# Weights stationary instead of tokens stationary in the last products of a two-layer MLP, with the result turned by VectorE

## The chip, the cores and the metric

The kernel runs on one NeuronCore of a Trainium2 chip. The metric is the device time of one execution, in microseconds, as the median of a few runs. The engines are TensorE (PE, with its weight loads as PEld), VectorE (DVE), ScalarE (ACT) and the DMA queue that SyncE (SP) issues. GpSimd does nothing here.

## What is computed

Three stages follow each other over 12160 tokens (2 sequences of 6080) with 256 features: a gated scan along the sequence, an MLP with squared ReLU, and an MLP with ELU. Both MLPs go 256 to 2048 to 256.

```python
f = lb + (1 - lb) * sigmoid(f_logit)
for t in range(S):                       # scan, per sequence and feature
    h = f[:, t] * h + (1 - f[:, t]) * x[:, t]
    y[:, t] = h
x1 = square(relu(y @ moe_w_in)) @ moe_w_out
out = elu(x1 @ moe2_w_in) @ moe2_w_out   # fp32 out, [12160, 256]
```

## The kernel before

**Precision.** Every fp32 operand of a product is split into a high part that TensorE's fp32r format holds and a low part that is the rest. A product is three matmuls: high by high, high by low, low by high.

**Tiling.** Tokens are cut into 24 blocks: one of 384, then 23 of 512 (`block_sizes`). In the code `m` is the MLP (0 or 1), called layer 1 and layer 2 here, `b` the block, `g` one of eight groups of 256 hidden features. A slot is one (m, b, g): first products (x by w_in, L611, in two parts "first" and "later", for a seven-product scheme on half blocks; L625 in the first four blocks of layer 1), the activation on ACT and DVE (lines 639 to 673), the split of the hidden values into `g` high (L678, ACT) and low (L683, DVE), and the second products (`out_mm`, L710), which accumulate over the eight groups in PSUM banks `acc`.

**Second products.** In layer 1 the output weights `wo[0]` are stationary and the 512 tokens of `g` move: per slot 2 hidden chunks x 2 halves of the 256 output features x 3 = 12 matmuls with 512 moving columns. In layer 2 the tokens are stationary (128 at a time) and the 256 columns of `wo[1]` move: per slot 2 x 4 x 3 = 24 matmuls with 256 moving columns (18 in the block of 384). So layer 2's result has tokens on partitions and can be stored as it is.

**Order on TensorE.** The order of PE steps is written out by hand: runs of two blocks of one layer are woven slot by slot, 16 slots to a run. Two runs of layer 1 begin, then runs of layer 2 and layer 1 alternate, and two runs of layer 2 end the kernel. So there are twelve layer-2 runs: a first one (blocks 0 and 1); nine (called the middle runs below) that alternate with layer 1; and a last two that follow each other. A slot's second products come three slots after its first products.

**Order on the other engines.** The class `Order` is a planner: each step has an engine, a cost in us, a due time and the buffers that it reads and writes; it plays the steps through at planning time, and on each engine takes the ready step with the earliest due time. What comes out is a fixed order per engine, in which each engine works strictly.

**After the second products.** `add_evacuation` gives, for each block, two steps per layer. For layer 1, ACT copies each `acc` bank (L775) and SP spills it to DRAM (L778). For layer 2, ACT copies each `acc` bank to a staging tile `o` (L790, two per block) and SP stores it to `out` (L794, rows of 1 KB). There are four `acc` banks (two blocks of a run in flight) and two `o` tiles. The scan (`add_scan`, L541 to L578) loads its inputs in DMAs of 64 KB, four per half block and tensor, and turns them with DVE's 32x32 block transposes (L550).

**Weights.** `add_weights` makes the parts of the output weights once per group: `high_part` (L402 on ACT or L404 on DVE) and `low_part` (L408, DVE), one instruction of 512 columns each.

Of the kernel before, what the change touches and what calls it, by code (L numbers as in the profile page):

```python
# [7 lines left out]
F32 = mybir.dt.float32  # L8
# [7 lines left out]
P = 128  # L16
# [138 lines left out]
def kernel(  # L155
# [24 lines left out]

    late = ctx.enter_context(tc.tile_pool(name="late", bufs=1))
    wo1 = late.tile([P, KF, 2, D], F32R, name="wo1")
    pools = {"ws": ctx.enter_context(tc.tile_pool(name="ws_pool", bufs=BUFS["ws"]))}
    const = ctx.enter_context(tc.tile_pool(name="const", bufs=1))
    lb = const.tile([P, KD], F32, name="lb")
# [1 line left out]
    gb = const.tile([P, KD], F32, name="gb")  # L189
    carry = const.tile([P, KD], F32, name="carry")  # L190
    warm = const.tile([P, 1], F32, name="warm")
    wo = [const.tile([P, KF, 2, D], F32R, name="wo0"), wo1]
    pools |= {
        tag: ctx.enter_context(tc.tile_pool(name=f"{tag}_pool", bufs=n))
        for tag, n in BUFS.items()
# [37 lines left out]
    def new(tag, shape, dtype=F32, name=None):  # L233
        return pools[tag].tile(shape, dtype, tag=name or tag, name=name or tag)
# [54 lines left out]
    def act(n, psum=False):  # L289
        return (0.05 if psum else 0.09) + n / 1172  # L290
# [68 lines left out]
    def add_weights(i, m, kind, c, due, wk=None):  # L359
        t = {}  # L360

        def load(e):
            t["st"] = new("st", [P, 2, CE // 2, 2], I32)
            load_w(nc.scalar if i == 0 else nc.sync, t["st"], m, kind, c)
            if i == 0:
                for k in range(KD):
                    nc.scalar.dma_start(lb[:, k : k + 1], lower_bound.rearrange("(q c i o) -> c q i o", q=4, c=KD, o=1)[k])
                nc.scalar.activation(warm, warm, AF.Exp)
            sv = t["st"].rearrange("p k e w -> p (k e) w")
            t["low"], t["high"] = sv[:, :, 0], sv[:, :, 1]  # L370

        def scaled(e):
            t["a"] = new("a", [P, 4, P])
            t["v"] = t["a"].rearrange("p q i -> p (q i)")
            t["vi"] = t["v"].bitcast(I32)
            nc.scalar.activation(t["v"], t["high"].bitcast(F32), AF.Abs, scale=2.0**-112)

        def low_bits(e):
            nc.scalar.activation(t["low"], t["low"].bitcast(U32), AF.Copy, scale=LOW_SCALE)

        def magnitude(e):
            nc.vector.scalar_tensor_tensor(t["vi"], t["vi"], 3, t["low"], op0=ALU.logical_shift_left, op1=ALU.bitwise_or)

        def sign(e):
            nc.vector.scalar_tensor_tensor(t["vi"], t["high"], -0x80000000, t["vi"], op0=ALU.bitwise_and, op1=ALU.bitwise_or)

        def sums(e):
            t["q"] = new("a", [P, 4, P])
            weight_sums(t["q"], t["a"])

        def parts():
            if kind == 0:
                return t["a"], ws_t[m, c][:, 0, 0:4], ws_t[m, c][:, 1, 0:4]
            v = t["a"].rearrange("p (k e) i -> p k (e i)", k=2)
            return v, *(wo[m][:, 2 * c : 2 * c + 2, x, :] for x in range(2))

        def high_part(e):
            if kind == 0:
                ws_t[m, c] = new("ws", [P, 2, NW, P], F32R)
            v, hi, _ = parts()  # L400
            if e == "ACT":
                nc.scalar.activation(hi, v, AF.Copy)  # L402
            else:
                nc.vector.tensor_copy(hi, v)  # L404

        def low_part(e):
            v, hi, lo = parts()
            nc.vector.tensor_tensor(lo, v, hi.bitcast(F32), op=ALU.subtract)  # L408

        def keep(e):  # L410
            nc.sync.dma_start(wd[m][c][:, :, 0:4].bitcast(F32), ws_t[m, c][:, :, 0:4].bitcast(F32))

        def keep_whole(e):
            nc.sync.dma_start(rd[c], t["a"])

        st, a = ("st", i), key_of("a")
        steps = [
            ["SP", 0.1 if i == 0 else 1.9 if m == 0 and kind == 0 else 0.475, load, (), [st], None, 512],
            ["ACT", act(CE), scaled, [st], [a]],
            ["ACT", act(CE), low_bits, (), [st]],  # L420
            ["DVE", dve(CE), magnitude, [st], [a]],
            ["DVE", dve(CE), sign, [st], [a]],
        ]
        if i == 0:
            order.add(*steps[0][:2], -20.0, *steps[0][2:])
            del steps[0]
        if m == 1 and kind == 0:
            q = key_of("a")
            chain(due - 6.0, [*steps, ["DVE", 4 * dve(P), sums, [a], [q]]])
            add_kept_parts(t, "a", a, m, c, 0, due - 2.0)  # L430
            add_kept_parts(t, "q", q, m, c, 4, due)
            return
        w = ("ws", wk) if kind == 0 else ("w", m, c)
        chain(due, [
            *steps,
            ["DVE", dve(CE, True), high_part, [a], [w], ("ACT", act(CE))],
            ["DVE", dve(CE), low_part, [a], [w]],
        ])
        if kind == 0:
            order.add("SP", 0.5, due + 6.0, keep, [w], [("wd", m, c, 0)], None, 512)  # L440
            order.add("SP", 0.5, due + 3.0, keep_whole, [a], [("rd", c)], None, 256)
# [160 lines left out]
    def add_slot(i, m, b, g, wk):  # L602
# [82 lines left out]
        def out_mm(e):  # L685
            begin, end = g == 0, g == KG - 1
            if begin:
                acc_t[m, b] = []
            for j in (2 * g + 1, 2 * g):
                d = 0 if j % 2 else 2 * n  # L690
                gh, gl = (t["g"][:, x, d : d + 2 * n] for x in range(2))
                one, two = begin and j % 2 == 1, end and j % 2 == 0
                for q in range(KD if m == 0 else 2 * n // P):
                    if m == 0:
                        if one:
                            acc_t[m, b].append(pa.tile([P, TB], F32, tag="acc", name="acc"))
                        a = acc_t[m, b][q][:, : 2 * n]
                        wh, wl = (wo[0][:, j, x, q * P : (q + 1) * P] for x in range(2))
                        three = ((wh, gh), (wh, gl), (wl, gh))
                        clear = one  # L700
                    else:
                        if one and q % 2 == 0:
                            acc_t[m, b].append(pa.tile([P, TB], F32, tag="acc", name="acc"))
                        a = acc_t[m, b][q // 2][:, q % 2 * D : (q % 2 + 1) * D]
                        vh, vl = (x[:, q * P : (q + 1) * P] for x in (gh, gl))
                        wh, wl = (wo[1][:, j, x, :] for x in range(2))
                        three = ((vh, wh), (vh, wl), (vl, wh))
                        clear = one and q % 2 == 0
                    for k, (u, v) in enumerate(three):
                        nc.tensor.matmul(a, lhsT=u, rhs=v, start=clear and k == 0, stop=two and k == 2, skip_group_check=True)  # L710

        na = KD if m == 0 else -(-2 * n // HB)
        if g == 0:
            t0 = acc_n[0]
            acc_n[0] += na
# [50 lines left out]
    def add_evacuation(m, b):  # L766
        n = sizes[b]
        due = out_due[m, b, KG - 1] + 12 * ROW * n + 4.0
        for q, key in enumerate(acc_k[m, b]):
            if m == 0:  # L770
                k = ("o", o_n[0] + q)

                def move(e, q=q):
                    o_t[m, b, q] = new("o", [P, 2, D])[:, :, : n // 2]
                    nc.scalar.activation(o_t[m, b, q], acc_t[m, b][q][:, :n].rearrange("p (h i) -> p h i", h=2), AF.Copy)  # L775

                def spill(e, q=q):
                    nc.sync.dma_start(xd[b][:, q], o_t[m, b, q])  # L778

                chain(due, [  # L780
                    ["ACT", act(n, True), move, [key], [k]],
                    ["SP", 0.5, spill, [k], [("xd", b, q)], None, n // 2],
                ])
            else:
                k = ("o", o_n[0] + q)
                w = min(2, n // P - 2 * q)

                def move(e, q=q, w=w):
                    o_t[m, b, q] = new("o", [P, 2, D])
                    nc.scalar.activation(o_t[m, b, q][:, :w], acc_t[m, b][q].rearrange("p (i e) -> p i e", i=2)[:, :w], AF.Copy)  # L790

                def store(e, q=q, w=w):
                    t0 = starts[b] + q * 2 * P
                    nc.sync.dma_start(out[t0 : t0 + w * P, :].rearrange("(i p) e -> p i e", p=P), o_t[m, b, q][:, :w])  # L794

                chain(due, [
                    ["ACT", act(w * D, True), move, [key], [k]],
                    ["SP", 0.5, store, [k], (), None, w * 128],
                ])
        o_n[0] += len(acc_k[m, b])  # L800

    def add_reload(b, due):
        n = sizes[b] // 2
# [97 lines left out]
```

## Time and profile before

| | us |
|---|---|
| median of 3 runs | 2113.92 (2113.29 to 2114.46) |
| profiled execution, its own time | 2113.18 |
| its span, first to last instruction | 2111.4 |

| engine | busy us | share of the span |
|---|---|---|
| PE | 2041.2 | 97% |
| PEld | 1925.7 | 91% |
| DVE | 1717.8 | 81% |
| ACT | 1692.7 | 80% |

The time outside the span is 1.8 us. Busy time of PE counts matmuls that overlap in the pipeline, so it is read here from starts: the distance from the first matmul of a group to the first of the next. The DVE's and ACT's instructions overlap their neighbours by some 0.08 us too. TensorE's granted clock is 0.997 of full speed over the run.

### The profile page before, as it was taken

The numbers are of one execution on the slowest core, as the hardware profiler recorded it, in microseconds if no ns is written. First come the engines' busy times: TensorE is split into PE (matmuls) and PEld (weight loads), VectorE is DVE, ScalarE is ACT, GpSimd is POOL, SyncE is SP. The second block draws the span as 40 slices with busy tenths as digits, with TensorE's granted clock in tenths as the row PEclk, the third lists the DMA queues.
The fourth block names the chain that finished last, engine by engine and source line by source line (L and its number), as shares of the span: only waits on it lengthen the run. The fifth ranks groups of instructions, "written<-read, shape, count | busy, mean of one in ns | idle before, by whom it ended". The sixth has DMA issues, their size and how long they took to land.

```text
span 2111.4 us, 36876 instructions
## 1 busy us (share of the span) xinstructions
PE 2041.2 (97%) x14640; PEld 1925.7 (91%) x14640; DVE 1717.8 (81%) x2833; ACT 1692.7 (80%) x2146; POOL 0.2 (0%) x4
## 2 busy tenths in 40 slices
PE   3999899999999999999999999999999999999998
PEld 2888889999899899999999989989999998999998
DVE  6977986986987887798698698789879859867886
ACT  5877787887788888788788888878878878878886
POOL 0000000000000000000000000000000000000000
PEclk8999999999999999999999999999999999999999
DMA  7877442432433433333243243333334324323231
GB/s 214 230 261 246 152 149 88 136 130 83 135 118 108 123 113 128 120 105 123 92 142 131 85 138 103 123 118 108 122 117 117 128 88 128 125 90 128 88 108 38
DMA packets 207539, 268.08 MB, mean 127 GB/s; under 512 B 110984, under 2 KB 135944, under 8 KB 207368
## 3 DMA queue, kind: packets, MB, share of 16 engines
q1 hardware_dynamic: 206784, 265.21, 39.9%
q8 instruction: 115, 1.88, 0.4%
q10 hardware_dynamic: 584, 0.53, 0.1%
q14 instruction: 56, 0.46, 0.1%
HBM read 221.91 MB, written 43.78 MB: 126 GB/s over the span
## 4 chain that ended last, share of the span: by engine, by line
PE 71%; DVE 20%; ACT 4%; DMA 2%; issue 2%; SPq 1%; DVEq 0%; ACTq 0%
PE acc L710 38%; PE pc L611 30%; DVE g L683 4%; PE pc L625 4%; DVE r L654 2%; DVE F L576 2%; DVE r L673 2%; DVE s L642 1%; DVE r L650 1%; DVE s L647 1%; DVE fT L559 1%; DMA xs<-in_x_dram 1%; DVE fT L550 1%; DVE xA L508 1%; DVE xT L562 1%
## 5 line engine op out<-in xcount | busy, mean ns | idle before, releaser
L710 PE MATMUL acc<-wo,g 128*128 128x256 f32 x4560 | 584.4, 283 | 20.2 <-DVE g L683 19.9
L710 PEld LDWEIGHTS acc<-wo,g 128*128 128x128 f32 x4560 | 561.3, 188 | 25.9 <-DVE g L683 25.2
L710 PE MATMUL acc<-g,wo 128*128 128x512 f32 (+1 forms) x2304 | 552.2, 389 | 0.0
L611 PE MATMUL pc<-xA,ws 128*128 128x256 f32 (+1 forms) x3696 | 486.1, 280 | 7.1 <-ACT s L639 7.1
L683 DVE TENSOR_TENSOR g<-r,g 128x1024 fp32r<-128x1024 f32 (+1 forms) x384 | 463.6, 1207 | 35.4 <-ACT g L678 34.3
L710 PEld LDWEIGHTS acc<-g,wo 128*128 128x128 f32 x2304 | 420.7, 188 | 78.1
L611 PE MATMUL pc<-xB,ws 128*128 128x256 f32 x3696 | 487.0, 281 | 3.9 <-ACT s L639 3.9
L611 PEld LDWEIGHTS pc<-xA,ws 128*128 128x128 f32 x3696 | 462.1, 188 | 17.0 <-ACT s L639 11.2
L611 PEld LDWEIGHTS pc<-xB,ws 128*128 128x128 f32 x3696 | 463.4, 188 | 11.0 <-ACT s L639 4.6
L678 ACT ACTIVATE g<-r 128x1024 fp32r<-128x1024 f32 (+1 forms) x384 | 403.1, 1050 | 58.3 <-DVE r L673 51.5
L647 DVE TENSOR_TENSOR s<-pc,s 128x256 f32<-128x256 f32 (+1 forms) x352 | 147.7, 420 | 283.5 <-PE pc L611 283.3
L639 ACT ACTIVATE s<-pc 128x768 f32<-128x768 f32 (+1 forms) x352 | 283.1, 804 | 48.8 <-PE pc L611 48.0
L673 DVE SCALAR_TENSOR_TENSOR r<-e,r 128x1024 f32<-128x1024 f32 (+1 forms) x192 | 231.2, 1204 | 22.7 <-ACT e L670 22.7
L654 DVE TENSOR_TENSOR r<-pc,s 128x512 f32<-128x512 f32 (+1 forms) x352 | 241.0, 685 | 7.7 <-ACT r L657 2.6
L657 ACT ACTIVATE r<-pc 128x256 f32<-128x256 f32 (+1 forms) x352 | 134.0, 381 | 112.5 <-DVE r L654 66.4
L660 ACT ACTIVATE r<-r 128x768 f32<-128x768 f32 x160 | 135.6, 847 | 105.3 <-DVE r L650 105.3
L667 ACT ACTIVATE e<-r 128x1024 f32<-128x1024 f32 (+1 forms) x192 | 201.2, 1048 | 19.0 <-DVE r L650 14.6
L663 ACT ACTIVATE r<-r 128x1024 f32<-128x1024 f32 (+1 forms) x192 | 202.1, 1053 | 5.4
L670 ACT ACTIVATE e<-e 128x1024 f32<-128x1024 f32 (+1 forms) x192 | 201.6, 1050 | 5.0
L642 DVE TENSOR_TENSOR s<-s 128x256 f32<-128x256 f32 (+1 forms) x352 | 147.4, 419 | 9.3 <-ACT s L639 0.7
L650 DVE TENSOR_TENSOR r<-s 128x256 f32<-128x256 f32 (+1 forms) x352 | 147.0, 418 | 0.0
L625 PE MATMUL pc<-xA,ws 128*128 128x384 f32 (+1 forms) x192 | 44.0, 382 | 23.2 <-DVE xA L502 22.9
(49 smaller groups left out, 849.5 us busy)
## 6 DMA issues: line engine op xcount, KB each, us to landing
ws<-wd SPq DMA_DIRECT2D x176, 896.0 KB, 5.0
out_dram<-o SPq DMA_DIRECT2D x47, 256.0 KB, 2.4
fs<-in_f_logit_dram SPq DMA_DIRECT2D x184, 64.0 KB, 2.4
xs<-in_x_dram SPq DMA_DIRECT2D x184, 64.0 KB, 2.8
xd<-o SPq DMA_DIRECT2D x46, 256.0 KB, 3.4
F<-xd SPq DMA_DIRECT2D x46, 256.0 KB, 5.0
st<-in_moe_w_out_dram SPq DMA_DIRECT2D x16, 512.0 KB, 4.9
wd<-wp SPq DMA_DIRECT2D x24, 256.0 KB, 4.7
```

What stands on the lines that cost most here:

```text
L611: nc.tensor.matmul(t["pc"][:, c], lhsT=ws[:, p, w], rhs=x_t[m, b][:, r, v], start=(which is FIRST_PRODUCTS and q == 0 and c in (1, 2)), st ...
L639: nc.scalar.activation(t["s"], t["pc"][:, 1:4], AF.Copy)
L642: nc.vector.tensor_tensor(t["s"][:, 1], t["s"][:, 1], t["s"][:, 2], op=ALU.add)
L647: nc.vector.tensor_tensor(t["s"][:, 0], t["pc"][:, 0], t["s"][:, 0], op=ALU.add)
L654: nc.vector.tensor_tensor(t["c"][:, 1:3], t["pc"][:, 2:4], u, op=ALU.add)
L663: nc.scalar.activation(t["r"], t["r"], AF.Square)
L667: nc.scalar.activation(t["e"], t["r"], AF.Relu, scale=-1.0)
L670: nc.scalar.activation(t["e"], t["e"], AF.Exp, scale=-1.0)
L673: nc.vector.scalar_tensor_tensor(t["r"], t["e"], 1.0, t["r"], op0=ALU.subtract, op1=ALU.max)
L678: nc.scalar.activation(t["g"][:, 0], t["r"], AF.Copy)
L683: nc.vector.tensor_tensor(t["g"][:, 1], t["r"], t["g"][:, 0].bitcast(F32), op=ALU.subtract)
L710: nc.tensor.matmul(a, lhsT=u, rhs=v, start=clear and k == 0, stop=two and k == 2, skip_group_check=True)
```

## The change

Layer 2's second products take the form of layer 1's: the weights `wo[1]` are stationary, the tokens of `g` move, 12 matmuls of 512 columns (384 in the first block) instead of 24 (18) of 256. The result then has features on partitions. For each block DVE transposes it from PSUM in blocks of 32x32, four instructions of 256 columns (two halves of the block, each from both `acc` banks), into the staging tile; ACT's two copies per block go away. So that a plain 32x32 block transpose gives 64 features in a row for a token, the columns of `wo[1]` are put in another order when they are made, in two instructions of 256 columns instead of one of 512 for each part. Each half of a block is stored by four DMAs of 64 KB with runs of 256 bytes, instead of one of 256 KB with runs of 1 KB. The tile `wo1` moves to another pool.

```diff
-                return t["a"], ws_t[m, c][:, 0, 0:4], ws_t[m, c][:, 1, 0:4]
+                return [(t["a"], ws_t[m, c][:, 0, 0:4], ws_t[m, c][:, 1, 0:4])]
             v = t["a"].rearrange("p (k e) i -> p k (e i)", k=2)
-            return v, *(wo[m][:, 2 * c : 2 * c + 2, x, :] for x in range(2))
+            hi, lo = (wo[m][:, 2 * c : 2 * c + 2, x, :] for x in range(2))
+            if m == 0:
+                return [(v, hi, lo)]
+            return [
+                (v[:, k].rearrange("p (a q j) -> p q a j", a=4, q=KD),
+                 *(u[:, k].rearrange("p (q a j) -> p q a j", a=4, q=KD) for u in (hi, lo)))
+                for k in range(2)
+            ]
...
-                    else:
-                        if one and q % 2 == 0:
-                            acc_t[m, b].append(pa.tile([P, TB], F32, tag="acc", name="acc"))
-                        a = acc_t[m, b][q // 2][:, q % 2 * D : (q % 2 + 1) * D]
-                        vh, vl = (x[:, q * P : (q + 1) * P] for x in (gh, gl))
-                        wh, wl = (wo[1][:, j, x, :] for x in range(2))
-                        three = ((vh, wh), (vh, wl), (vl, wh))
-                        clear = one and q % 2 == 0
+                for q in range(KD):
+                    if one:
+                        acc_t[m, b].append(pa.tile([P, TB], F32, tag="acc", name="acc"))
+                    a = acc_t[m, b][q][:, : 2 * n]
+                    wh, wl = (wo[m][:, j, x, q * P : (q + 1) * P] for x in range(2))
+                    for k, (u, v) in enumerate(((wh, gh), (wh, gl), (wl, gh))):
+                        nc.tensor.matmul(a, lhsT=u, rhs=v, start=one and k == 0, stop=two and k == 2, skip_group_check=True)
...
-                def move(e, q=q, w=w):
-                    o_t[m, b, q] = new("o", [P, 2, D])
-                    nc.scalar.activation(o_t[m, b, q][:, :w], acc_t[m, b][q].rearrange("p (i e) -> p i e", i=2)[:, :w], AF.Copy)
-                def store(e, q=q, w=w):
-                    t0 = starts[b] + q * 2 * P
-                    nc.sync.dma_start(out[t0 : t0 + w * P, :].rearrange("(i p) e -> p i e", p=P), o_t[m, b, q][:, :w])
+                def turn(e, h=q):
+                    o_t[m, b, h] = o = new("o", [P, HB // 32, KD, 32])[:, : n // 64]
+                    for c in range(KD):
+                        v = acc_t[m, b][c][:, h * n // 2 : (h + 1) * n // 2]
+                        nc.vector.transpose(o[:, :, c], v.rearrange("p (n i) -> p n i", i=32))
+                def store(e, h=q):
+                    t0 = starts[b] + h * n // 2
+                    v = out[t0 : t0 + n // 2, :].rearrange("(n j) (a u) -> a j n u", j=32, a=4)
+                    for a in range(4):
+                        nc.sync.dma_start(v[a], o_t[m, b, h][32 * a : 32 * a + 32].rearrange("j n c i -> j n (c i)"))
                 chain(due, [
-                    ["ACT", act(w * D, True), move, [key], [k]],
-                    ["SP", 0.5, store, [k], (), None, w * 128],
+                    ["DVE", 2 * dve(n // 2), turn, accs, [k]],
+                    ["SP", 1.9, store, [k], (), None, n // 2],
                 ])
```

## Rows read from the trace of the kernel before

**Rows 1.** Page, part 1: busy us (share of the span) x instructions.

```profile
PE 2041.2 (97%) x14640; PEld 1925.7 (91%) x14640; DVE 1717.8 (81%) x2833; ACT 1692.7 (80%) x2146; POOL 0.2 (0%) x4
```

**Rows 2.** Page, part 4: the chain that ended last, share by engine.

```profile
PE 71%; DVE 20%; ACT 4%; DMA 2%; issue 2%; SPq 1%; DVEq 0%; ACTq 0%
```

**Rows 3.** Groups by shape: busy us, mean ns of one, idle before and its releaser.

```profile
L710 PE MATMUL acc<-wo,g 128*128 128x256 f32 x4560 | 584.4, 283 | 20.2 <-DVE g L683 19.9 <-ACT g L678 0.3
L710 PE MATMUL acc<-g,wo 128*128 128x512 f32 x2208 | 535.1, 391 | 0.0
...
L647 DVE TENSOR_TENSOR s<-pc,s 128x256 f32<-128x256 f32 x344 | 144.9, 421 | 282.2 <-PE pc L611 282.0
L642 DVE TENSOR_TENSOR s<-s 128x256 f32<-128x256 f32 x344 | 144.5, 420 | 8.6
...
L550 DVE STREAM_TRANSPOSE xT<-xs 128x512 f32<-128x512 f32 x46 | 32.3, 702 | 0.0
```

**Rows 4.** Timeline of PE in a layer-1 run: start us, us, line, matmuls merged.

```profile
333.24 2.91 PE L710 MATMUL acc<-g,wo 128*128 128x512 f32 x12
335.99 1.57 PE L611 MATMUL pc<-xA,ws 128*128 128x256 f32 x12
...
348.88 1.32 PE L710 MATMUL acc<-g,wo 128*128 128x512 f32 x5
```

**Rows 5.** Timeline of PE in a middle layer-2 run.

```profile
1109.73 3.04 PE L710 MATMUL acc<-wo,g 128*128 128x256 f32 x24
1112.61 1.58 PE L611 MATMUL pc<-xA,ws 128*128 128x256 f32 x12
...
1125.84 3.04 PE L710 MATMUL acc<-wo,g 128*128 128x256 f32 x24
```

**Rows 6.** Waits of the engines: total us, times, longest us.

```profile
PE acc L710 <- DVE g L683: 19.9, 26, 1.0
```

**Rows 7.** Busy us of each engine in stretches: length, PE, PEld, DVE, ACT.

```profile
214.00:307.00 93.00, 84.22 (x692) 82.05 (x691) 91.60 (x169) 72.14 (x102) 0.00 (x0) 1.00 0.49 150
...
461.00:481.00 20.00, 20.00 (x164) 19.73 (x163) 19.11 (x31) 18.37 (x26) 0.00 (x0) 1.00 0.44 148
481.00:533.00 52.00, 52.00 (x331) 47.07 (x330) 29.44 (x51) 40.51 (x51) 0.00 (x0) 1.00 0.25 89
533.00:576.00 43.00, 41.56 (x285) 38.13 (x283) 42.76 (x76) 34.87 (x46) 0.00 (x0) 1.00 0.53 148
...
1941.00:2091.00 150.00, 150.00 (x1260) 150.00 (x1259) 120.41 (x179) 121.61 (x148) 0.00 (x0) 1.00 0.26 89
```

**Rows 8.** Timeline of PE where a layer-2 run begins, with idle before.

```profile
576.75 2.89 PE L710 MATMUL acc<-wo,g 128*128 128x256 f32 x22 [1.02 <-DVE g L683]
```

**Rows 9.** Timeline of DVE where that layer-2 run's predecessor ended.

```profile
465.16 0.41 DVE L642 TENSOR_TENSOR s<-s 128x256 f32<-128x256 f32 x1
465.49 0.42 DVE L650 TENSOR_TENSOR r<-s 128x256 f32<-128x256 f32 x1
...
471.70 0.69 DVE L484 TENSOR_TENSOR F<-F 128x512 f32<-128x512 f32 x1
...
483.84 0.42 DVE L647 TENSOR_TENSOR s<-pc,s 128x256 f32<-128x256 f32 x1 [2.29 <-PE pc L611]
```

**Rows 10.** Timeline of all engines at the end of the kernel.

```profile
2104.71 2.89 PE L710 MATMUL acc<-wo,g 128*128 128x256 f32 x22 [0.75 <-DVE g L683]
2106.93 1.31 ACT L790 ACTIVATE o<-acc 128x512 f32<-128x512 f32 x2 [3.53 <-PE acc L710]
2107.56 1.08 SPq L794 DMA_DIRECT2D out_dram<-o  x2
```

**Rows 11.** Waits of SP's queue: total us, times, longest us.

```profile
SPq L468 <- PE pc L611: 1099.3, 135, 12.2
```

**Rows 12.** Timeline of SP: four 64 KB loads of the scan, issued in a row.

```profile
566.01 1.79 SPq L541 DMA_DIRECT2D xs<-in_x_dram  x4
```

**Rows 13.** Page, part 6: DMA issues, KB each, us from issue to landing.

```profile
fs<-in_f_logit_dram SPq DMA_DIRECT2D x184, 64.0 KB, 2.4
```

More of the change, by code (lines that the diff above doesn't have):

```diff
@@ L179 @@
     NBK = len(sizes)
-    late = ctx.enter_context(tc.tile_pool(name="late", bufs=1))
-    wo1 = late.tile([P, KF, 2, D], F32R, name="wo1")
     pools = {"ws": ctx.enter_context(tc.tile_pool(name="ws_pool", bufs=BUFS["ws"]))}
@@ L191 @@
     warm = const.tile([P, 1], F32, name="warm")
-    wo = [const.tile([P, KF, 2, D], F32R, name="wo0"), wo1]
+    wo = [const.tile([P, KF, 2, D], F32R, name=f"wo{m}") for m in range(2)]
     pools |= {
@@ L399, in high_part @@
                 ws_t[m, c] = new("ws", [P, 2, NW, P], F32R)
-            v, hi, _ = parts()
-            if e == "ACT":
-                nc.scalar.activation(hi, v, AF.Copy)
-            else:
-                nc.vector.tensor_copy(hi, v)
+            for v, hi, _ in parts():
+                if e == "ACT":
+                    nc.scalar.activation(hi, v, AF.Copy)
+                else:
+                    nc.vector.tensor_copy(hi, v)
         def low_part(e):
-            v, hi, lo = parts()
-            nc.vector.tensor_tensor(lo, v, hi.bitcast(F32), op=ALU.subtract)
+            for v, hi, lo in parts():
+                nc.vector.tensor_tensor(lo, v, hi.bitcast(F32), op=ALU.subtract)
         def keep(e):
@@ L692, in out_mm @@
                 one, two = begin and j % 2 == 1, end and j % 2 == 0
-                for q in range(KD if m == 0 else 2 * n // P):
-                    if m == 0:
-                        if one:
-                            acc_t[m, b].append(pa.tile([P, TB], F32, tag="acc", name="acc"))
[L697 to L701, printed above, removed]
-                        if one and q % 2 == 0:
-                            acc_t[m, b].append(pa.tile([P, TB], F32, tag="acc", name="acc"))
-                        a = acc_t[m, b][q // 2][:, q % 2 * D : (q % 2 + 1) * D]
-                        vh, vl = (x[:, q * P : (q + 1) * P] for x in (gh, gl))
-                        wh, wl = (wo[1][:, j, x, :] for x in range(2))
-                        three = ((vh, wh), (vh, wl), (vl, wh))
-                        clear = one and q % 2 == 0
-                    for k, (u, v) in enumerate(three):
-                        nc.tensor.matmul(a, lhsT=u, rhs=v, start=clear and k == 0, stop=two and k == 2, skip_group_check=True)
-        na = KD if m == 0 else -(-2 * n // HB)
+                for q in range(KD):
[5 more added lines that the diff above has]
+                        nc.tensor.matmul(a, lhsT=u, rhs=v, start=one and k == 0, stop=two and k == 2, skip_group_check=True)
+        na = KD
         if g == 0:
@@ L768, in add_evacuation @@
         due = out_due[m, b, KG - 1] + 12 * ROW * n + 4.0
-        for q, key in enumerate(acc_k[m, b]):
+        accs = acc_k[m, b]
+        for q in range(KD):
+            k = ("o", o_n[0])
+            o_n[0] += 1
             if m == 0:
-                k = ("o", o_n[0] + q)
                 def move(e, q=q):
@@ L780, in add_evacuation @@
                 chain(due, [
-                    ["ACT", act(n, True), move, [key], [k]],
+                    ["ACT", act(n, True), move, [accs[q]], [k]],
                     ["SP", 0.5, spill, [k], [("xd", b, q)], None, n // 2],
@@ L784, in add_evacuation @@
             else:
-                k = ("o", o_n[0] + q)
-                w = min(2, n // P - 2 * q)
-                def move(e, q=q, w=w):
-                    o_t[m, b, q] = new("o", [P, 2, D])
-                    nc.scalar.activation(o_t[m, b, q][:, :w], acc_t[m, b][q].rearrange("p (i e) -> p i e", i=2)[:, :w], AF.Copy)
-                def store(e, q=q, w=w):
-                    t0 = starts[b] + q * 2 * P
-                    nc.sync.dma_start(out[t0 : t0 + w * P, :].rearrange("(i p) e -> p i e", p=P), o_t[m, b, q][:, :w])
+                def turn(e, h=q):
[8 more added lines that the diff above has]
+                        nc.sync.dma_start(v[a], o_t[m, b, h][32 * a : 32 * a + 32].rearrange("j n c i -> j n (c i)"))
                 chain(due, [
-                    ["ACT", act(w * D, True), move, [key], [k]],
-                    ["SP", 0.5, store, [k], (), None, w * 128],
+                    ["DVE", 2 * dve(n // 2), turn, accs, [k]],
+                    ["SP", 1.9, store, [k], (), None, n // 2],
                 ])
-        o_n[0] += len(acc_k[m, b])
     def add_reload(b, due):
```

## The prediction

> **What bounds the kernel now.** First the page's parts 1 and 4. TensorE is busy 97% of the span, DVE 81%, ACT 80% [rows 1], and the chain that ended last lies 71% on PE and 20% on DVE [rows 2]. So PE sets the time over most of the span, and DVE in some stretches. The timeline of PE says what a slot costs where nothing stalls it. In a layer-1 run three slots go from 333.24 to 348.88, which is 5.213 us each [rows 4]; in a layer-2 run from 1109.73 to 1125.84, 5.370 us each [rows 5]. Both slots hold the same 21 first products; the second products take 2.75 us in layer 1 (333.24 to 335.99) and 2.88 us in layer 2 (1109.73 to 1112.61), though both move 6144 columns. So a matmul of 512 columns goes by in 229 ns and two of 256 in 240: 11 ns or so are paid per instruction, not per column.
>
> Then the stretches [rows 7]. In 481 to 533, the calm part of a layer-1 run, DVE is busy 29.4 of 52 us. In 533 to 576, where a layer-1 run ends and a layer-2 run begins, it is busy 42.8 of 43: the scans of two later blocks are squeezed in there. PE stalls in that stretch for DVE's low parts: 26 times, 19.9 us in the whole run [rows 6], of which two stalls fall at the start of each of the nine middle layer-2 runs; [rows 8] is one of them. In 461 to 481, where a layer-2 run ends, DVE is busy 19.1 of 20 us, yet PE 20.0 of 20: full, but in time. The first layer-2 run (214 to 307) is held up by DVE, 91.6 of 93 us busy, with PE at 84. In the last two layer-2 runs DVE has 30 us to spare in 150.
>
> **The matmuls.** With the change a layer-2 slot has on PE what a layer-1 slot has now: 12 matmuls of 512 columns with `wo` stationary and `g` moving, and the same 21 first products. So where PE sets the pace I expect 5.213 in place of 5.370 us, 0.157 us less per slot. As bound from below I take the second products' own difference, 0.13 us (24 matmuls of 2.88 against 12 of 2.75); the rest of 0.157 is at the joints to the neighbouring products, and should come along, since the joints too are those of layer 1.
>
> How many slots gain? Of 192, the first run's 16 are DVE's (next part). In each of the nine middle runs two slots stall for DVE; there a faster PE only waits longer, so 14 of 16 count: 126. Of the last 32 the final three wait for the closing chain of activations: 29. Together 155 x 0.157 = 24.3 us. With 0.13 us it is 20.2; with 11 slots per middle run, if the stalls spread, 128 x 0.157 = 20.1.
>
> [...] The row shows a fixed cost of some 11 ns per matmul [rows 4, 5]. [...]
>
> **The evacuation.** ACT loses two copies per block (1.31 us at the end of the kernel) [rows 10]. That gives nothing where PE sets the pace, and I count it at nothing. DVE gets four transposes of 256 columns per block. The trace has transposes of 512 columns from SBUF: 702 ns busy [rows 3], like DVE's other 512-column work. A DVE instruction of 256 columns takes 420 ns, the same from PSUM (L647, 421) as from SBUF (L642, 420) [rows 3], and 0.33 us from start to start in a row of them [rows 9]. I take 0.34 us for one transpose, so 1.36 us per block and 2.7 per run; upper end 0.63 us, nearly a 512-column one, 2.5 per block and 5.0 per run. A reason for less than 0.33 I don't see.
>
> [...]
>
> Where do they lie? A run's first block ends three slots before the run does, so its transposes come up near 461, at the start of the stretch with DVE 19.1 of 20 busy [rows 7]; those of its second block at 478, just before DVE falls idle for 2.29 us in each slot [rows 9]. The second are hidden. The first push DVE's queue back by up to 1.36 us. Behind them wait the sums L647 to L654, the low parts L683 and the parts of the next blocks' x; PE waits for the low parts. The planner knows the new step and puts what is due last behind: the differences L484 to L492 that it does here [rows 9] are input parts of the next layer-2 run, some 70 us off, and can go into the 2.29 us holes after 481. So I take 0.17 us per middle run, 1.5 us together; bounds 0 and 2.7 per run. Neither the four `acc` banks nor the two `o` tiles should bind: the next user of either comes some 16 us later.
>
> **The first run.** DVE is full there, so what is added to DVE is added to the time, and the matmuls give nothing. Block 0 (384) has four transposes of 192 columns, about 0.27 us each, 1.1; block 1 has 1.36; the two last pairs of weight parts, 0.33 us more each, 0.7. Together 3.1 at most; the transposes of block 1 come at its end, before the slack of layer 1, so I take 2 (0 to 3.1). The other weight parts, six pairs, are made before 214, where DVE has holes: nothing; if not, 2 us.
>
> **Stores.** SP issues 192 small DMAs of 64 KB instead of 48. Four such in a row take it 1.79 us [rows 12], so a block costs it 3.6 us instead of about 1. SP spends 1099 us waiting for a `ws` buffer to come free [rows 11], so it has room, and a 64 KB load lands in 2.4 us [rows 13]. Hidden, except at the end.
>
> **The end.** Now PE stops at 2107.60, the last copy and store follow [rows 10], and the span ends 3.8 us after PE. The last store is issued about 0.7 us after PE stops, so 3.1 us are its landing and the close. After the change the first half's two transposes take 0.76 us; then eight issues of 0.45 us [rows 12], the second half's transposes beside them; the last begins at 0.8 + 7 x 0.45 = 3.9 us, and with 3.1 more the end is 7.0 us after PE: 3.2 us more.
>
> **Sum.** -24.3 + 2 (first run) + 1.5 (run ends) + 3.2 (end) = -17.6. Against the profiled execution, 2113.18, that is 2095.6. The median of the runs shown is 0.7 above it, so the forecast is 2096.
>
> **Rivals.** (a) DVE takes PE's place at the end of each middle run: the transposes fit into no hole, and both blocks' 2.7 us land on the path. For it: 19.1 of 20 us are busy in 461 to 481. Against: 2.29 us holes right behind, and work there that isn't due. Price: 9 x 2.7 = 24.3 in place of 1.5, so -24.3 + 2 + 24.3 + 3.2 = +5.2, 2119; with transposes at 0.63 us 9 x 5.0 = 45, 2140. It decides from (24.3 - 5.2)/9 = 2.1 us lost per middle run. (b) The same in part: 0.6 to 1.7 us per middle run, 2100 to 2110, most likely 2105. (c) TensorE's time goes by columns, and layer 2's 0.157 us come from something that stays: then no gain, only 2 + 1.5 + 3.2, 2121. Against it: [rows 4] shows the same instruction form at work. [...] (d) SP's longer stores delay a weight load behind them, or a staging tile comes free late and DVE, which works strictly in order, stands before its transpose: 1 us per middle run, 9 us, 2105. Against it: SP mostly waits.
>
> **Chances.** Forecast 0.68 (2089 to 2102), (a) 0.08, (b) 0.12, (c) 0.05, (d) 0.07. Bounds of the forecast: all 24.3 with no loss but the end's 3.2 gives 2093; its extra joints (two stalled slots gaining too, 2.8 us) 2090. With 20.1 gained and 3.1, 5 and 3.2 lost it is 2105. Range 2088 to 2109, which takes in (b) and (d) and leaves out (a) and (c). A measurement of this kernel can tell about 0.2% from no change, 4.2 us: faster is below 2109.7, slower above 2118.1. Faster: the forecast's 0.68 and 0.17 of the 0.19 of (b) and (d), 0.85. Same: the other 0.02, and 0.05 from (a) and (c) where they come out milder, 0.07. Slower: the remaining 0.08 of (a) and (c).
>
> **What would show it.** Right: PE's slots at 5.21 us in layer-2 runs, at `out_mm` 4416 matmuls of 512 columns and none of 256; transposes from `acc` at 420 ns; stalls for L683 still at the starts of middle runs, a little longer each. Wrong: slots above 5.3 us (the fixed cost isn't what I read); new PE stalls of over 1 us in front of second products near the end of layer-2 runs (case a or b); DVE idle with its transpose waiting for a store, or PE for `ws` (case d); more than 8 us between PE's last matmul and the end.

## The result, and the profile after

| | before | after |
|---|---|---|
| median, us | 2113.89 | 2093.07 |
| runs, us | 2113.29 to 2114.46 | 2092.28 to 2093.78 |
| profiled execution, its own time, us | 2113.18 | 2093.78 |
| its span, us | 2111.4 | 2092.0 |

The ratio is 0.9902 with a 95% interval of 0.9886 to 0.9918: 20.8 us or 1.0% less. The forecast was 2096, the range 2088 to 2109.

The page's parts 1 and 4 after (busy us and share; chain by engine), against [rows 1, 2]:

```profile
PE 2016.1 (96%) x12384; PEld 1804.3 (86%) x12384; DVE 1738.5 (83%) x2929; ACT 1682.4 (80%) x2114; POOL 0.2 (0%) x4
...
PE 70%; DVE 22%; ACT 4%; issue 2%; DMA 2%; SPq 1%; DVEq 0%; ACTq 0%
```

PE has 2256 matmuls fewer, and DVE is busy 21 us more. Groups by shape after, against [rows 3] (busy us, mean ns, idle before and its releaser):

```profile
L706 PE MATMUL acc<-g,wo 128*128 128x512 f32 x4416 | 1077.6, 392 | 18.8 <-DVE g L690 17.7 <-ACT g L685 1.0
...
L649 DVE TENSOR_TENSOR s<-s 128x256 f32<-128x256 f32 x344 | 143.9, 418 | 8.0 <-ACT s L646 0.4
...
L788 DVE STREAM_TRANSPOSE o<-acc 128x256 f32<-128x256 f32 x92 | 33.3, 417 | 2.8 <-PE acc L706 2.8
```

No product of 256 columns is left at `out_mm`, and a transpose of 256 columns from PSUM takes 417 ns busy, as the 256-column rows L647 (421) and L642 (420) had it. Timeline of PE after, in one of the last two layer-2 runs, against [rows 5]:

```profile
2022.14 2.91 PE L706 MATMUL acc<-g,wo 128*128 128x512 f32 x12
2024.89 1.57 PE L618 MATMUL pc<-xA,ws 128*128 128x256 f32 x12
...
2027.36 2.91 PE L706 MATMUL acc<-g,wo 128*128 128x512 f32 x12
...
2032.57 2.91 PE L706 MATMUL acc<-g,wo 128*128 128x512 f32 x12
```

Two slots take 2032.57 - 2022.14 = 10.43 us, 5.21 each, where [rows 5] has 5.37: the slot of a layer-1 run [rows 4].

**Where the time went**, run by run of TensorE's order: the length of a run is taken on the timeline of PE from the first of its second products to the first of the next run's.

| part | before | after | difference |
|---|---|---|---|
| from the span's start to the first second product | 49.6 | 50.4 | +0.8 |
| first layer-2 run | 93.35 | 93.29 | -0.1 |
| each of nine middle layer-2 runs | 88.02 | 85.93 | -2.1 (9 x: -18.8) |
| each layer-1 run between (the last one: 83.4 in both) | 84.3 | 84.3 | 0 |
| last two layer-2 runs, to PE's last matmul | 85.92 + 80.23 | 83.41 + 78.69 | -4.0 |
| from PE's last matmul to the span's end | 3.79 | 6.77 | +3.0 |

With 0.3 us less in the layer-1 runs this makes the 19.4 us between the spans. The 0.8 us at the start isn't the change's: the kernel before and six of those below, five of which open as the changed one does, have 49.2 to 50.1 there.

### The profile page after: what moved, and what is told of

Its sections match the earlier page's. It is cut to its first block, busy times and chain, and to the rows that moved or that the text cites. A ratio compares the mean times of both kernels' runs of the same rounds, so it can differ in the third digit from the quotient of the medians.

```text
span 2092.0 us, 32599 instructions
## 1 busy us (share of the span) xinstructions
PE 2016.1 (96%) x12384; PEld 1804.3 (86%) x12384; DVE 1738.5 (83%) x2929; ACT 1682.4 (80%) x2114; POOL 0.2 (0%) x4
## 4 chain that ended last, share of the span: by engine, by line
PE 70%; DVE 22%; ACT 4%; issue 2%; DMA 2%; SPq 1%; DVEq 0%; ACTq 0%
PE acc L706 37%; PE pc L618 29%; DVE g L690 4%; PE pc L632 4%; DVE r L661 3%; DVE F L583 2%; DVE r L680 2%; DVE s L649 2%; DVE r L657 1%; DVE s L654 1%; DVE fT L566 1%; DVE fT L557 1%; DVE xA L515 1%; DVE xT L569 1%; DVE xB L515 1%
## 5 line engine op out<-in xcount | busy, mean ns | idle before, releaser
L706 PE MATMUL acc<-g,wo 128*128 128x512 f32 (+1 forms) x4608 | 1113.8, 390 | 23.1 <-DVE g L690 21.8
L706 PEld LDWEIGHTS acc<-g,wo 128*128 128x128 f32 x4608 | 839.2, 188 | 186.9 <-DVE g L690 30.3
L690 DVE TENSOR_TENSOR g<-r,g 128x1024 fp32r<-128x1024 f32 (+1 forms) x384 | 463.1, 1206 | 32.1 <-ACT g L685 30.5
L618 PEld LDWEIGHTS pc<-xA,ws 128*128 128x128 f32 x3696 | 466.7, 188 | 24.2 <-ACT s L646 11.2
L649 DVE TENSOR_TENSOR s<-s 128x256 f32<-128x256 f32 (+1 forms) x352 | 146.7, 417 | 8.7 <-ACT s L646 1.1
L632 PE MATMUL pc<-xA,ws 128*128 128x384 f32 (+1 forms) x192 | 44.5, 386 | 23.1 <-DVE xA L509 22.8
L583 DVE TENSOR_TENSOR_SCAN F<-fT,carry,xT 128x256 f32<-128x256 f32 (+2 forms) x94 | 64.2, 723 | 0.0
L632 PEld LDWEIGHTS pc<-xA,ws 128*128 128x128 f32 x192 | 37.6, 202 | 28.1 <-ACT st L377 22.8
```

The source lines that it names most:

```text
L618: nc.tensor.matmul(t["pc"][:, c], lhsT=ws[:, p, w], rhs=x_t[m, b][:, r, v], start=(which is FIRST_PRODUCTS and q == 0 and c in (1, 2)), st ...
L649: nc.vector.tensor_tensor(t["s"][:, 1], t["s"][:, 1], t["s"][:, 2], op=ALU.add)
L690: nc.vector.tensor_tensor(t["g"][:, 1], t["r"], t["g"][:, 0].bitcast(F32), op=ALU.subtract)
L706: nc.tensor.matmul(a, lhsT=u, rhs=v, start=one and k == 0, stop=two and k == 2, skip_group_check=True)
```

## The experiments

Each kernel ran on one chip beside the kernel before, whose median was 2113.4 to 2114.2 each time. "After" is the changed kernel, "before" the kernel before.

**Is it the number of instructions, or which operand is stationary?** The changed kernel, with each 512-column product cut in two:

```diff
-                    for k, (u, v) in enumerate(((wh, gh), (wh, gl), (wl, gh))):
-                        nc.tensor.matmul(a, lhsT=u, rhs=v, start=one and k == 0, ...)
+                    for i in range(1 + m):
+                        w = 2 * n // (1 + m)
+                        z = slice(i * w, i * w + w)
+                        for k, (u, v) in enumerate(((wh, gh), (wh, gl), (wl, gh))):
+                            nc.tensor.matmul(a[:, z], lhsT=u, rhs=v[:, z], start=one and k == 0 and i == 0, ...)
```

> The changed kernel with each of layer 2's 512-column second products split into two of 256 columns (first and second half of the tokens), weights still stationary: 24 matmuls per slot again, nothing else changed. Theory (a fixed cost of some 11 ns per matmul, so the number of instructions counts): layer-2 slots back at 5.37 us, nine middle runs back at 88.0 us, the time 2093 + 9 x 2.1 + 2.5 + 1.9 = 2116 us. Rival A (the gain comes from which operand is stationary, so that freshly written tokens need not be loaded as weights) and rival B (it comes from ACT being relieved of the copies): slots stay at 5.21, 2093 us.

Measured 2113.55 us, ratio to before 0.9998 (0.9988 to 1.0007). Timeline of PE of this kernel, in a late layer-2 run:

```profile
2035.13 3.04 PE L709 MATMUL acc<-g,wo 128*128 128x256 f32 x24
2038.00 1.57 PE L618 MATMUL pc<-xB,ws 128*128 128x256 f32 x12
...
2040.47 3.04 PE L709 MATMUL acc<-g,wo 128*128 128x256 f32 x24
...
2045.81 3.04 PE L709 MATMUL acc<-g,wo 128*128 128x256 f32 x24
```

The 24 matmuls take 2.87 us again, against 2.88 in the kernel before and 2.75 for 12 of double width. The kernel is back at the time of the one before, though weights are stationary and ACT is relieved, so neither rival explains the gain. The theory's 2116 was 2.5 us too high: a slot is 5.34 us ((2045.81 - 2035.13) / 2), not 5.37. So about 0.13 of the 0.157 us per slot belong to the number of instructions. Each matmul here has a weight load of its own (x12384 for PE and PEld alike after), and both were doubled in layer 2 (at `out_mm` x6912 of each here, x4608 after), so these runs don't tell which of the two has the fixed cost. The other 0.03 stay gained: they lie mostly in the 21 first products, 2.47 us here and after, 2.49 behind tokens that are stationary [rows 5]. Why those go faster behind weights was not tried.

**Is it ACT's relief, and what do the transposes cost?** The changed kernel with ACT's copies in place of the transposes:

```diff
-                ["DVE", 2 * dve(n // 2), turn, accs, [k]],
-                ["SP", 1.9, store, [k], (), None, n // 2],
+                ["ACT", act(n, True), move, [accs[q]], [k]],
+                ["SP", 0.5, store, [k], (), None, n // 2],
```

> The changed kernel without DVE's transposes: ACT copies each acc bank as it did, SP stores the copy in one DMA per half. Left out: the turning of layer 2's result, so features and tokens stand untransposed in the output. Theory (the gain is TensorE's, the transposes are hidden except at the kernel's end): middle layer-2 runs stay at 85.9 us within 0.2, the end after PE's last matmul goes from 6.8 back to 3.8 us and the last chain loses 0.6, time 2089 to 2090. Rival B (the gain is ACT's relief): middle runs near 88, time near 2110. Rival C (the transposes cost PE 0.5 us or more per middle run): 2085 or less.

Measured 2089.76 us, 3.3 less than after. Timeline of PE in a middle layer-2 run, then of all engines at the end:

```profile
600.74 2.91 PE L706 MATMUL acc<-g,wo 128*128 128x512 f32 x12
...
611.17 1.09 PE L706 MATMUL acc<-g,wo 128*128 128x512 f32 x4
```

```profile
2081.38 2.79 PE L706 MATMUL acc<-g,wo 128*128 128x512 f32 x11 [0.76 <-DVE g L690]
2083.53 1.28 ACT L786 ACTIVATE o<-acc 128x512 f32<-128x512 f32 x2 [3.46 <-PE acc L706]
2084.15 1.01 SPq L791 DMA_DIRECT2D out_dram<-o  x2
```

Slots are 5.215 us with the copies on ACT, middle runs 85.9 us as after. So ACT's relief gives nothing, and the transposes cost nothing in the middle runs. They cost at the end: without them the last run is 0.4 us shorter, and 3.6 us follow PE's last matmul instead of 6.8.

**The evacuation alone, on the kernel before:**

```diff
-                    ["ACT", act(w * D, True), move, [key], [k]],
-                    ["SP", 0.5, store, [k], (), None, w * 128],
+                    ["DVE", 2 * dve(n // 2), turn, acc_k[m, b], [k]],
+                    ["SP", 1.9, store, [k], (), None, n // 2],
```

> The kernel before with only the evacuation changed: on blocks of 512 of layer 2 DVE transposes from acc and four stores per half replace ACT's copies; the products stay as they were. The output's layout is then not the reference's (each 32x32 block of the already token-major result is turned). Theory: middle layer-2 runs stay at 88.0 us, the end costs 3.0 us more and the last chain up to 0.6, time 2117 to 2118. Rival B (ACT's relief is the gain): under 2105. Rival C (transposes cost 0.5 us per run or more): 2122 or more.

Measured 2116.92 us, ratio 1.0014 (1.0004 to 1.0023): 2.8 us more than before. Middle runs stay at 88.0 us, the end is 6.9 us after PE, the last run 0.3 longer. The two halves of the change add up: beside the 2114.15 of the kernel before, measured next to both, the products alone (the kernel with ACT's copies above) are -24.4 and the evacuation alone +2.8, together -21.6, against -20.8 for the change.

**How much cover is left?** Each transpose done twice:

```diff
-                    for c in range(KD):
+                    for c in (0, 1, 0, 1):
...
-                    ["DVE", 2 * dve(n // 2), turn, accs, [k]],
+                    ["DVE", 4 * dve(n // 2), turn, accs, [k]],
```

> The changed kernel with every transpose done twice (eight instead of four per block), and the planner told so: 2.7 us more DVE work per layer-2 run. It measures how much cover is left for them. Theory (work that is not due moves into DVE's holes behind the run's end): middle runs longer by 0 to 0.4 us each, the end by 2 to 3 us (eight transposes and the last chain), time 2095 to 2100. Rival (a) of the prediction, DVE full at the end of each layer-2 run so that each added us lands on the path: 9 x 2.7 us and the end, 2117 to 2120.

Measured 2103.46 us, 10.4 more than after. Timeline of DVE and of PE of this kernel at the end of a middle layer-2 run:

```profile
461.92 2.76 DVE L788 STREAM_TRANSPOSE o<-acc 128x256 f32<-128x256 f32 x8
477.65 2.76 DVE L788 STREAM_TRANSPOSE o<-acc 128x256 f32<-128x256 f32 x8
```

```profile
473.90 0.39 PE L706 MATMUL acc<-g,wo 128*128 128x512 f32 x1
474.45 2.79 PE L706 MATMUL acc<-g,wo 128*128 128x512 f32 x11 [0.16 <-DVE g L690]
...
479.55 2.68 PE L706 MATMUL acc<-g,wo 128*128 128x512 f32 x11
```

2.7 us of added DVE work lengthen a middle run by 0.45 us (86.4 against 85.9), in its last slot, 5.65 us (473.90 to 479.55): PE now waits for a low part at 474.45. So at the first price the cover just sufficed, and the second is mostly covered too; rival (a) falls. The theory's 2095 to 2100 was too low: nine middle runs give 4.1 us, the one before the last 0.5, the first run 2.0 and the last run with the end 3.0. The middle runs and the end lie at or just beyond the upper end of what was expected of them; the first run's 2.0 the theory had left out.

**The end.** The last block's stores on two queues:

```diff
-                        nc.sync.dma_start(v[a], ...)
+                        queue = nc.scalar if b == NBK - 1 and a % 2 else nc.sync
+                        queue.dma_start(v[a], ...)
```

> The changed kernel with the last block's eight stores issued alternately on SP's and ACT's queue. Theory (the eight issues of 0.45 us one behind the other make up most of the longer end): the last store starts 2.1 instead of 3.9 us after PE's last matmul, the end goes from 6.8 to about 5.1 us, time 1.7 us less, 2091.3. Rival (the landing of the 256-byte runs sets the end): no change, 2093.

Measured 2091.62 us, 1.5 less than after, with a ratio to before of 0.9897 (0.9883 to 0.9912), an interval that overlaps that of after; it is the profile that tells them apart. Timeline of all engines at the end of this kernel, then the time from issue to landing of the last four stores, here and after:

```profile
2080.91 2.79 PE L706 MATMUL acc<-g,wo 128*128 128x512 f32 x11 [0.77 <-DVE g L690]
...
2084.22 1.98 SPq L795 DMA_DIRECT2D out_dram<-o  x4
2084.22 2.03 ACTq L795 DMA_DIRECT2D out_dram<-o  x4
```

```profile
DMA to landing us min/median/max: 2.6/2.7/2.7
...
DMA to landing us min/median/max: 1.8/1.9/1.9
```

The span ends 5.6 us after PE's last matmul instead of 6.8. So the row of eight issues is part of the longer end, 1.2 us, less than the 1.7 expected. The issues went as the theory had them: the last one starts 2.0 us after PE's last matmul instead of 3.9. But the stores land 2.7 us after their issue, where they took 1.9, so the landing, which the rival named, gives 0.8 us back. Why they land later was not tried.

**What holds PE at the start of each middle run?** There part of the gain was lost: 2.1 of 16 x 0.157 = 2.5 us per run came through. Two kernels try to win back the stalls. First a third `F` buffer (with `wp`, `st` and `a` cut by one each to make room):

```diff
-    "fs": 1, "xs": 1, "fT": 1, "xT": 1, "F": 2, "xA": 1, "xB": 1, "ws": 4, "wp": 3, "r": 3, "e": 1,
-    "g": 3, "s": 2, "st": 3, "a": 5, "o": 2, "pc": 2, "acc": 4,
+    "fs": 1, "xs": 1, "fT": 1, "xT": 1, "F": 3, "xA": 1, "xB": 1, "ws": 4, "wp": 2, "r": 3, "e": 1,
+    "g": 3, "s": 2, "st": 2, "a": 4, "o": 2, "pc": 2, "acc": 4,
```

> The changed kernel with three instead of two F buffers, so that the scan of the next blocks can begin before the layer-2 blocks' parts are made; to make room, buffers used while weights are made in the first 300 us are cut by one each (wp, st, a). Theory (the stalls at the start of each middle layer-2 run, 3.4 us with the slot before it, come from scans squeezed between the release of F and the next layer-1 run): most of them vanish, 9 x 2 to 3.4 us, with up to 5 us lost in the preparation, time 2062 to 2080. Rival (the scan is held back by something else): no change in the middle runs, 2093 to 2098.

Measured 2088.76 us, above the 2062 to 2080 expected. A middle layer-2 run falls from 85.93 to 83.75 us, but a layer-1 run rises from 84.3 to 84.7. That is 1.8 us per pair of runs, less than the 2 to 3.4 expected: the stalls at the start shrink, but 0.4 us come back in the layer-1 run. And the opening, up to the end of the first layer-2 run, is 11.2 us longer (319.1 against 307.9), where 5 were allowed for. That the preparation's missing buffers do this is likely, but was not tried apart. Then less DVE work in that stretch:

```diff
-            for c in range(KD):
+            for c in range(KD if b < PLAIN else 0):
...
-            ["DVE", 2 * dve(n, True), gate, (), [fT]],
+            ["DVE", 2 * dve(n, True) if b < PLAIN else 0.0, gate, (), [fT]],
```

> The changed kernel without DVE's gate instructions (fT = fT * ga + gb) from the fifth block on; left out: the mapping of tanh to the forget gate, so the scan runs on other numbers. 2.9 us less DVE work per pair of blocks in the stretch where DVE is full. Theory (the first slots of a middle layer-2 run are set by DVE, so TensorE's gain is lost there): the excess of 3.4 us per middle run falls to 0.5 to 1, time 2093 - 9 x 2.6 = 2070 (2066 to 2078). Rival (these stalls come from an order of buffers, not from DVE's work): within 3 us of 2093.

Measured 2094.59 us: a miss. 2.9 us less DVE work per pair of blocks bought nothing. Layer-2 runs got 0.8 us shorter (85.1), layer-1 runs 0.9 longer (85.2): the stalls moved to other slots. Busy us in the same stretch, after and without gates (columns as in [rows 7]):

```profile
532.00:574.00 42.00, 40.79 (x258) 36.20 (x256) 41.76 (x75) 33.33 (x44) 0.00 (x0) 1.00 0.52 150
```

```profile
532.00:574.00 42.00, 39.15 (x242) 34.74 (x242) 41.66 (x72) 32.84 (x45) 0.00 (x0) 1.00 0.52 151
```

DVE is as full with less to do: the planner puts other work that is ready into the room. So a full DVE is no proof that the amount of its work sets the time. What PE waits for shows on DVE's timeline after:

```profile
572.54 1.39 DVE L583 TENSOR_TENSOR_SCAN F<-fT,carry,xT 128x256 f32<-128x256 f32 x2
573.96 0.17 DVE L585 COPY carry<-F 128x2 f32<-128x2 f32 x1
574.04 1.22 DVE L690 TENSOR_TENSOR g<-r,g 128x1024 fp32r<-128x1024 f32 x1
```

and on PE's:

```profile
575.31 2.81 PE L706 MATMUL acc<-g,wo 128*128 128x512 f32 x11 [1.13 <-DVE g L690]
```

The low part L690, for which PE stands idle for 1.13 us, is behind a scan step of the next blocks (572.54 to 574.04, 1.5 us), which is not due for long. The planner has the scan at 0.9 us and the gate at 0.40, where the rows have 1.5 and 0.65 (two gate instructions, 568.56 to 569.20 after): four half blocks make 3.4 us per pair, about what is lost. A new theory, tried with nothing but the two costs:

```diff
-            ["DVE", 2 * dve(n, True), gate, (), [fT]],
+            ["DVE", 2 * dve(n), gate, (), [fT]],
...
-            ["DVE", dve(N) + 0.3, scan, ...],
+            ["DVE", 2 * dve(N) + 0.3, scan, ...],
```

> The changed kernel with two of the planner's costs set to what the trace shows: the scan step 1.5 us per half block (562.00 to 563.50 in the changed kernel) where the planner had 0.9, the gate step 0.67 where it had 0.40. No instruction is added or left out, only the order on the engines can differ. Theory D (formed after the run without gates: the 3.4 us of stalls at the start of each middle layer-2 run come from the order, in which low parts that PE waits for stand behind scan steps that the planner took for 0.9 us cheaper per half, 3.6 us per pair of blocks): the stalls shrink by 1.5 to 3.4 us per run, 9 times, time 2063 to 2080. Rival E (there is too little DVE time between the release of F and the next due products, whatever the order): within 4 us of 2093.

Measured 2066.68 us, ratio to before 0.9778 (0.9762 to 0.9794). The same stretch, then PE's waits for low parts, after and here, and the start of a middle layer-2 run:

```profile
532.00:574.00 42.00, 41.80 (x262) 37.41 (x262) 41.75 (x74) 36.50 (x48) 0.00 (x0) 1.00 0.49 145
```

```profile
PE acc L706 <- DVE g L690: 21.8, 25, 1.4
...
PE acc L706 <- DVE g L690: 4.7, 8, 0.8
```

```profile
560.44 2.91 PE L706 MATMUL acc<-g,wo 128*128 128x512 f32 x12
...
565.65 3.33 PE L706 MATMUL acc<-g,wo 128*128 128x512 f32 x12
...
571.29 2.91 PE L706 MATMUL acc<-g,wo 128*128 128x512 f32 x12
```

DVE is as full, 41.75 of 42, and PE waits 4.7 us in the whole execution for low parts where it waited 21.8 after. (The run begins 7.4 us earlier in this kernel; the stretch moved by as much, 524.6 to 566.6, has 41.75 too.) Layer-2 runs are 84.2 us, layer-1 runs 83.41, the first layer-2 run 91.1. So most of the stalls came from the plan, and rival E falls.

The plan changed in one thing beside the order, which the theory didn't expect: casts of `xB` went from DVE to ACT, one per pair of runs. DVE's group, after and here:

```profile
L509 DVE CAST xB<-F 128x1024 fp32r<-128x1024 f32 x12 | 8.1, 674 | 3.0 <-PE pc L632 3.0
...
L509 DVE CAST xB<-F 128x1024 fp32r<-128x1024 f32 x3 | 2.1, 686 | 0.0
```

That is 0.7 us of DVE work less per pair, where a pair got 2.6 us shorter, and taking away 2.9 us of work had bought nothing. So the order has the larger part; what the cast adds, and which of the two costs counts, was not tried apart. The next kernel joins this to the two queues:

> The same costs, and the last block's eight stores issued alternately on SP's and ACT's queue. Theory: 1.5 us below the run with the costs alone, since only the end differs; with theory D 2062 to 2078, with rival E 2088 to 2095.

Measured 2064.66 us, ratio 0.9769 (0.9754 to 0.9783), 2.0 below the costs alone (5.7 us after PE's last matmul, against 6.8): the fastest here, 28 us below the changed kernel. Last, the costs on the kernel before:

> The kernel before, with the same two planner costs set right and nothing else changed. If the stalls belong to the planner's order and not to the products' form, the kernel before loses them too: 2.5 to 3 us per middle run, to about 88.0 - 1.5 + 0.2 = 86.7 us for a layer-2 run and 83.4 for a layer-1 run, time 2086 to 2091, and the change on top of it (2066.7 with the costs) is worth 20 to 24 us: TensorE's gain in up to 16 slots of each middle run. Rival (with slower products the same low parts are late again): 2105 or more, and the two edits are worth more together than the sum.

Measured 2087.11 us, ratio 0.9877 (0.9861 to 0.9894). Its middle layer-2 runs are 86.3 us, its layer-1 runs 83.4. The same edit takes 26.5 us from the kernel before and 26.4 from the changed one, and the change is worth 20.4 us on top of it, 20.8 without it. That the costs recover as much on two kernels with different plans speaks against a lucky arrangement, and it adds to the change's gain instead of being part of it.

## Why the prediction was right, point by point

**The matmuls.** Right, and so was its place: the slot fell to 5.21 us wherever PE sets the pace, and cutting the matmuls in two took the gain back: 12 more instructions for the same columns cost 2.87 - 2.75 = 0.12 us, 10 ns each, where some 11 were read from [rows 4, 5]. Of the 0.157 us, though, 0.03 are not this fixed cost, as I half said with "the joints": they are in the first products.

**How many slots.** 14 of 16 per middle run were counted, 2.2 us; 2.09 were measured, 13.3 slots. The last two runs gave 4.0 instead of 4.55, mostly because the transposes of the block before the last one delay the closing chain: a slot there takes 3.5 us after, 2.9 before, and 3.1 with ACT's copies.

**The first run.** This step failed. +2 us were forecast from "DVE is full there, so what is added to DVE is added to the time"; measured -0.1. DVE groups of that run (93 us; busy us, mean ns, idle before), two after, then two before:

```profile
L788 DVE STREAM_TRANSPOSE o<-acc 128x192 f32<-128x192 f32 (+1 forms) x8 | 2.6, 382 | 0.0
L491 DVE TENSOR_TENSOR F<-F 128x512 f32<-128x512 f32 x3 | 2.0, 682 | 0.0
...
L484 DVE TENSOR_TENSOR F<-F 128x512 f32<-128x512 f32 x4 | 2.7, 687 | 0.0
L502 DVE CAST xB<-F 128x1024 fp32r<-128x1024 f32 x1 | 0.7, 686 | 0.0
```

The 2.6 us of transposes are there. But the differences L491 run three times in it, where the kernel before has four (with the two small ones that go with them 1.5 us), and the cast of 0.7 us went over to ACT: work that wasn't due left the run. Nor does taking the transposes away shorten it: with ACT's copies it takes 93.7 us. With the transposes doubled it did get 2.0 us longer, so the room was about one set of transposes.

**The ends of the middle runs.** 1.5 us were allowed for, nothing was lost. DVE and the idle gap behind, after, against [rows 9]:

```profile
460.88 1.44 DVE L788 STREAM_TRANSPOSE o<-acc 128x256 f32<-128x256 f32 x4
...
476.08 1.44 DVE L788 STREAM_TRANSPOSE o<-acc 128x256 f32<-128x256 f32 x4
...
482.39 0.42 DVE L654 TENSOR_TENSOR s<-pc,s 128x256 f32<-128x256 f32 x1 [0.77 <-PE pc L618]
```

The transposes stand where the prediction put them and cost 1.36 us to the next start (460.88 to 462.24), the first idle gap shrank from 2.29 to 0.77 us. Their price held too: 417 ns for the transposes from PSUM, 418 for the 256-column instructions L649 from SBUF.

**The starts of the middle runs.** The size was right: two slots gain little or nothing, and PE's waits for low parts got a little longer, 21.8 us against 19.9 [rows 6], as forecast. The reason was not. I read them as DVE having too much to do, because it was busy 42.8 of 43 us [rows 7]. It is just as busy with most of the stalls gone. The failed step is "the scans of two later blocks are squeezed in there": they were put in front of due work, by a plan that took them for cheaper than they are, and with two costs set right PE waits 4.7 us for low parts instead of 21.8.

**The end.** +3.2 forecast, +3.0 measured:

```profile
2082.42 2.79 PE L706 MATMUL acc<-g,wo 128*128 128x512 f32 x11 [0.76 <-DVE g L690]
2084.57 0.45 DVE L788 STREAM_TRANSPOSE o<-acc 128x256 f32<-128x256 f32 x1 [2.21 <-PE acc L706]
2085.25 1.11 DVE L788 STREAM_TRANSPOSE o<-acc 128x256 f32<-128x256 f32 x3 [0.23 <-PE acc L706]
2085.73 3.86 SPq L794 DMA_DIRECT2D out_dram<-o  x8
```

Eight issues take 3.86 us in a row. The first transpose starts before PE's last matmul ends (the bank of the first 128 features is done 0.6 us earlier), which the prediction had not used.

**Sum.** -24.3 + 2 + 1.5 + 3.2 = -17.6 against -22.8 - 0.1 + 0 + 3.0 = -19.9. The 3.6 us that weren't lost at DVE and 0.2 at the end, less 1.5 that the matmuls gave less, are 2.3 of the 2.9 us by which the forecast was too high; the rest is the spread between executions. So it came this close partly by luck: the terms for DVE and the one for the matmuls erred in opposite directions.

## What to carry to other kernels

Where TensorE sets the pace, look at the starts of two forms of the same product in one trace: at equal columns, half as many instructions of twice the width were 0.12 us per 6144 columns cheaper, and which operand is stationary can be chosen for that, if another engine has room to turn the result. An engine that is busy for all of a stretch need not be what limits it: under a planner it fills with work that isn't due (DVE was 41.66 of 42 us busy with 2.9 us of its work taken away), and the test is to change the order, or the costs that the plan is made from, and not only the work. Compare a planner's costs with the durations in the trace; two wrong ones were worth more here than the change.

## What the runs showed of the hardware that wasn't expected

The 21 products that follow a group with tokens stationary take 2.49 us, behind a group with weights stationary 2.47, whether that group has 24 or 12 matmuls; no cause was tried. Two queues that issue stores side by side start the last one 1.9 us earlier, but the last four then take 2.7 us from issue to landing, where on one queue they take 1.9. A 32x32 block transpose by DVE took 417 ns from PSUM for 256 columns, what an elementwise instruction of that size took (L649 from SBUF, 418).
